# Loading q four tokens to a partition in a retention and MLP kernel

## The chip, the cores and the metric

The kernel runs on one core of a Trainium2 chip. The metric is the device time of one execution in microseconds (us); the median of several executions is used. The core has a matrix engine (PE), a vector engine (DVE), an engine for activations (ACT), a general one (POOL) and a queue engine (SP) that computes nothing and issues transfers. Each works through its own instructions in order; semaphores tie them together. Transfers are issued by SP, ACT or POOL and carried out by 16 DMA engines which all queues share.

## The reference: what is computed

```python
scores = scale * np.matmul(q, k.transpose(0, 1, 3, 2))        # scale = 1/8; q, k, v: [8, 8, 576, 64]
gamma = 1.0 - 2.0 ** (-5.0 - np.arange(H, dtype=np.float32))
rel = pos[:, None] - pos[None, :]
Dmat = np.where(rel >= 0, gamma[:, None, None] ** rel[None, :, :], 0.0)
attn = np.matmul(scores * Dmat[None, :, :, :], v)             # retention: causal, with a decay for each head
x = attn.transpose(0, 2, 1, 3).reshape(4608, 512)
h = x @ w_in                                                  # 512 -> 2048
out = (h * np.cos(h)) @ w_out                                 # 2048 -> 512
```

Inputs and output are float32; the kernel multiplies in bf16.

## The kernel before

**The retention part.** Each of 8 batches is cut into five pieces of 128 tokens (r = 0 to 3) and 64 (r = 4); here a pair (b, r) names one. Since the decay between two tokens is a product of a factor of the one and a factor of the other, q is multiplied by the table UQ, v by the table WV (`decay`, L311), and k is only cast to bf16 (`kcast`, L304). `load` (L273) brings k, q or v of a piece from memory into the float32 tiles kn, qn, vn: heads 0 to 3 lie in partitions 0 to 63, heads 4 to 7 in 64 to 127, and each partition holds ns consecutive tokens of a head (2, or 1 for r = 4). So a half of the load, one DMA, moves 64 partitions x 4 heads in runs of 512 bytes, and each load is two DMAs on SP (L281).

k and q of a piece must also stand with the 64 head elements in the partitions. In batches 0 and 1 PE transposes them (`turn`, L338; ACT copies them out, L348); from batch 2 on one DMA transpose issued by SP does it (`prep_dma`, L326, issue at L332). `scores` (L372) multiplies k and q, 16 small matmuls to a piece, into two PSUM banks sc, and DVE multiplies them by a causal mask MK (L389). `rest` (L394) multiplies these by v and, for r > 0, adds q times the state of the pieces before (ps<-kqt,sb); then it adds the piece's own k times v for the state. ACT copies the result out of PSUM into XT (L439), where it stands with d_model in the partitions and the tokens side by side: here the order of the tokens is put right. `state` (L444) adds to the float32 state on DVE (L453) and makes its bf16 copy on ACT (L456).

**The MLP part.** The 4608 tokens are nine blocks of 512. `mlp1` (L466) makes a block's 16 tiles of hidden values on PE, their cosine on ACT (L482) and the product on DVE (L485). `layer2` (L584) multiplies by w_out in seven products of 2 x 2 sub-blocks (fewer products, more sums on DVE), and stores.

**What sets the order.** The order is written out by hand in `emit` (L678). The start (L680 to L792) treats batches 0 and 1 and the first blocks. It issues all loads of batch 0, builds constants (`consts`, L227), and fills PE with matmuls on zeros (`idle`, L366) where it would wait, 12 of them first. The four loads of w_in and four of w_out are on POOL's queue; the first waits for v of (0, 0), the second for q of (0, 2), the third for q of (0, 3). From then on block j's `mlp1` tiles alternate with `layer2`. The retention of batch j+1 is put into the products of `layer2(j)` at the steps VISITS = 0, 3, 6, 9, 12: at each, `rest` of the piece before and `scores` of the next. The preparation is earlier: `prep_dma` of batch j+1, r = 2, 3, 4, in the `mlp1` tiles of block j and of batch j+2, r = 0, 1, in `layer2(j)`. In each, POOL casts k and multiplies q and v (L308, L317), SP issues the transpose, and then `loads_to` (L671) puts behind it on SP the next loads in order, so that before the transpose of (b, r) the loads of pieces 0 to 5b + r + 2, that is 5b + r + 3 pieces, have been issued, at least the 15 issued before the first transpose.

**Constants.** POOL's iotas write the token numbers IP and the differences MI for the mask (L239), DVE corrects the upper half (L243) and compares for the mask (L251); DVE zeroes the identity matrix and POOL puts in the ones (L246); ACT's exponentials make UQ and WV, one for each table and head, 16 in all (L260). PE's first transposes need the identity matrix, the first q decay (on DVE) needs UQ.

Of the kernel before, what the change touches and what calls it, by code (L numbers as in the profile page):

```python
# [6 lines left out]
ALU = mybir.AluOpType  # L7
# [7 lines left out]
NP = H_ // 2  # L15
# [28 lines left out]
def ns_of(r):  # L44

    return ck_of(r) // 64


# [92 lines left out]
class _Kernel:  # L141
    def __init__(self, nc, es, q, k, v, w_in, w_out, out):
# [52 lines left out]
        self.bOSB = [Buf() for _ in range(4)]  # L195
        self.IP = sb("ip", [128, NIP], F32)
        self.WV = sb("wv", [128, NIP * 4], F32)
        self.UQ = sb("uq", [128, NIP * 4], F32)
# [6 lines left out]
        self.C_PIH = sb("c_pih", [128, 1], F32)  # L205
        self.bIP, self.bWV, self.bUQ, self.bMK, self.bC, self.bID, self.bIDLE = (Buf() for _ in range(7))

# [19 lines left out]
    def consts(self):  # L227
        s = self.s
        s.op("dve", lambda e: e.memset(self.C_LN8.ap(), float(math.log(1.0 / 8.0))), writes=[Buf()])
        s.op("dve", lambda e: e.memset(self.C_PIH.ap(), float(math.pi / 2.0)), writes=[self.bC])  # L230
        s.op("dve", lambda e: e.memset(self.IDLE.ap(), 0.0), writes=[self.bIDLE])
        self.touch(AF.Exp)

        for t, b, o, n, pat, base, mul in (
                (self.IP, self.bIP, 0, NIP, [[CH, NCH - 1], [1, 2]], 0, 2),
                (self.IP, self.bIP, NIP - 1, NIP, [[0, 1]], CH * (NCH - 1), 1),
                (self.MI, self.bMK, 0, 2 * CH, [[-1, 2], [1, 2], [2, 64]], 0, -2)):
            shape = [[n, 128]] + [[1, 1]] if o else [[n, 128], [1, n - 1]] if n == NIP else [[n, 128], [128, 2], [64, 2], [1, 64]]
            s.op("pool", lambda e: e.iota(bass.AP(t, o, shape), pat, base=base, channel_multiplier=mul,  # L239
                                          allow_small_or_imprecise_dtypes=True), writes=[b])  # L240
        for o, n in ((0, NIP - 1), (NIP - 1, 1)):
            up = bass.AP(self.IP, 64 * NIP + o, [[NIP, 64], [1, n]])
            s.op("dve", lambda e: e.tensor_scalar(up, up, -128.0 if n > 1 else -64.0, None, ALU.add),  # L243
                 reads=[self.bIP], writes=[self.bIP])
# [12 lines left out]
        for t, b, sign in ((self.UQ, self.bUQ, 1.0), (self.WV, self.bWV, -1.0)):  # L257
            for h in range(H_):
                hs, hh = divmod(h, 4)
                s.op("act", lambda e: e.activation(  # L260
                    bass.AP(t, 64 * hs * 4 * NIP + hh, [[4 * NIP, 64], [4, NIP]]),
                    bass.AP(self.IP, 64 * hs * NIP, [[NIP, 64], [1, NIP]]), AF.Exp, scale=sign * self.lng[h],
                    **(dict(bias=bass.AP(self.C_LN8, 64 * hs, [[1, 64], [1, 1]])) if sign > 0 else {})),
                    reads=[self.bIP, self.bC], writes=[Buf()])
            b.w = [Tok("act", "act", s.count["act"], {})]

# [6 lines left out]
    def load(self, x, b, r, after=()):  # L273
        ns = ns_of(r)
        t, bt = self.ST32[x][r], self.bST32[x][r]

        def half(hs):
            dst = bass.AP(t, 64 * hs * 256 * ns, [[256 * ns, 64], [D_ * ns, 4], [1, D_ * ns]])
# [3 lines left out]

        return self.s.dma("sp", f"{x}n{r}", [half(0), half(1)], writes=[bt], after=after)

# [26 lines left out]
    def decay(self, eng, x, b, r):  # L311
        ns, i = ns_of(r), b % 2
        if x == "q":
            o, bt, w, bw = self.by_head(self.KQ[i][r], 256 * ns, 512 * ns, ns, D_, 256), self.bQB[i][r], self.UQ, self.bUQ
        else:
            o, bt, w, bw = self.by_head(self.VB[i][r], 0, 256 * ns, ns, D_ * ns, D_), self.bVB[i][r], self.WV, self.bWV
        self.s.op(eng, lambda e: e.tensor_tensor(  # L317
            o, self.by_head(self.ST32[x][r], 0, 256 * ns, ns, D_ * ns, D_),
            bass.AP(w, r * 8, [[4 * NIP, 128], [1, 4], [4, ns], [0, D_]]), ALU.mult),
            reads=[self.bST32[x][r], bw], writes=[bt])  # L320

# [50 lines left out]
    def scores(self, b, r):  # L372
# [3 lines left out]
        for c in range(2):  # L376
            for sl in range(ns):
                for hs in range(2):
                    for hp in range(2):
# [3 lines left out]
                            bass.AP(self.KQT[i], k0 + sl * 256, [[W, 64], [1, 64]]),  # L383
                            bass.AP(self.KQT[i], k0 + 256 * ns, [[W, 64], [256, ns], [1, 64]]),
                            dict(start=c == 0 and sl == 0, stop=c == 1 and sl == ns - 1, skip_group_check=True)))
        self.group(mms, [self.bKT[i][r], self.bQT[i][r]], self.bSC)
        for hp in range(2):
            p3 = [[512, 128], [ns * nq, 2], [1, ns * nq]]
            s.op("dve", lambda e: e.tensor_tensor(  # L389
                bass.AP(self.RT[r % 2][hp], 0, p3), bass.AP(self.SC[hp], 0, p3),  # L390
                bass.AP(self.MK, 0, [[2 * CH, 128], [0, 2], [1, ns * nq]]), ALU.mult),
                reads=[self.bSC[hp], self.bMK], writes=[self.bRT[r % 2][hp]])

    def rest(self, b, r, state=True):  # L394
# [39 lines left out]
        n0 = min(ck, XR - t0)  # L434
        for x0, po0, n in ((t0, 0, n0), (0, n0 // ns, ck - n0)):
            if n:
                o = bass.AP(self.XT, x0, [[NP * XR, 128], [XR, NP], [1, ns], [ns, n // ns]])
                p = bass.AP(self.PS, po0, [[1024, 128], [256, NP], [64, ns], [1, n // ns]])
                s.op("act", lambda e: e.activation(o, p, AF.Copy),  # L439
# [408 lines left out]
```

## Time and profile before

| | us |
|---|---|
| median of 3 runs | 309.16 (308.28 to 310.27) |
| the profiled execution's own time | 309.18 |
| its span, first to last instruction | 307.1 |
| PE busy | 292.3 |
| DVE busy | 232.3 |
| ACT busy | 190.1 |
| POOL busy | 115.8 |
| q's load issues on SP: 80, median of one | 0.617 |
| DMA transposes on SP: 30, median of one | 1.282 |

Times in the trace count from the start of the span. A line of a timeline gives the start, the time taken, the engine, the line of the kernel, the operation with its tiles, how many instructions were merged into it, and in brackets the idle time before it and what ended that. `SPq` is SP's queue; its issues are not counted as busy. A line of a source (L281 and so on) gives the least, the median and the longest time of one instruction in ns, then the first and last start. In a line of groups, the numbers after the first bar are the busy time in us and the mean of one instruction in ns, after the second bar the idle time of the engine just before and what ended it. Matmuls are pipelined, so that the time shown for one is longer than what it adds.

### The profile page before, as it was taken

What the parts mean: (1) busy time and instruction counts of PE and PEld (TensorE: products, weight loads), DVE (VectorE), ACT (ScalarE), POOL (GpSimd) and SP (SyncE); (2) the same over time, 40 slices, a digit from 0 to 9 for tenths busy, and PEclk for the clock granted to TensorE, in tenths of its full rate; (3) what the DMA queues carried; (4) which work ended last, traced back from release to release, by engine and by line L of the source; (5) the groups of instructions that cost most, each with busy time, mean ns of one, the idle gap of its engine ahead of it and who ended that gap; (6) DMA issues with size and microseconds to landing.
All of it is one profiled execution on the core that took longest, in us unless ns stands there. A gap on an engine that the chain in (4) does not pass through costs nothing.

```text
span 307.1 us, 8716 instructions
## 1 busy us (share of the span) xinstructions
PE 292.3 (95%) x3520; PEld 190.6 (62%) x3520; DVE 232.3 (76%) x393; ACT 190.1 (62%) x336; POOL 115.8 (38%) x133
## 2 busy tenths in 40 slices
PE   8768997999899999999999999999999999999996
PEld 3347644553587458746874687457845874685485
DVE  3347654867986898789878986999689768937963
ACT  6647845587565766576657665865576657724730
POOL 2346271999835444533551445436341000000000
PEclk9969999999999999999999999999999999999999
DMA  4999999567986987697879799977795012003003
GB/s 137 204 203 218 215 235 235 156 162 198 235 177 184 280 129 189 169 269 161 164 180 260 160 174 170 290 168 173 191 254 97 2 50 89 2 0 130 10 0 140
DMA packets 103480, 49.60 MB, mean 162 GB/s; under 512 B 45456, under 2 KB 98960, under 8 KB 103440
## 3 DMA queue, kind: packets, MB, share of 16 engines
q1 hardware_dynamic: 94176, 35.80, 54.2%
q10 hardware_dynamic: 5040, 9.05, 8.8%
q0 software_dynamic: 4224, 4.19, 8.4%
q8 instruction: 28, 0.46, 0.6%
q14 instruction: 12, 0.10, 0.1%
HBM read 36.70 MB, written 9.44 MB: 150 GB/s over the span
## 4 chain that ended last, share of the span: by engine, by line
PE 82%; DVE 5%; ACT 4%; SPq 4%; DMA 2%; issue 1%; POOL 0%; DVEq 0%; ACTq 0%
PE mm L362 59%; PE mm L364 14%; PE ps L362 6%; SPq L281 4%; PE sc L362 3%; DMA kn<-in_k_dram 2%; ACT cb L482 2%; DVE gt L485 1%; DVE ss L542 1%; DVE rt L389 1%; ACT sb L456 1%; ACT xt L439 1%; ACT kqt L348 1%; DVE ss L485 1%; DVE s L453 0%
## 5 line engine op out<-in xcount | busy, mean ns | idle before, releaser
L362 PE MATMUL mm<-xt,win 128*128 128x512 bf16 (+5 forms) x517 | 119.0, 349 | 2.0 <-DVE gt L485 1.2
L482 ACT ACTIVATE cb<-mm,c_pih 128x512 bf16<-128x512 f32 (+3 forms) x147 | 98.7, 680 | 33.7 <-PE mm L364 30.0
L485 DVE TENSOR_TENSOR gt<-mm,cb 128x512 bf16<-128x512 f32 (+1 forms) x130 | 85.7, 678 | 11.8 <-ACT cb L482 8.2
L362 PEld LDWEIGHTS mm<-xt,win 128*128 128x128 bf16 x517 | 46.8, 99 | 49.5 <-ACT cb L482 4.0
L364 PE MATMUL mm<-xt,win 128*128 128x512 bf16 (+5 forms) x147 | 54.0, 368 | 0.0
L389 DVE TENSOR_TENSOR rt<-sc,mk 128x512 bf16<-128x512 f32 (+1 forms) x80 | 44.8, 601 | 11.4 <-PE sc L364 11.4
L308 POOL CAST kq<-kn 128x512 bf16<-128x512 f32 (+1 forms) x40 | 25.2, 629 | 66.3 <-DMA kn<-in_k_dram 66.3
L317 POOL TENSOR_TENSOR kq<-qn,uq 128x512 bf16<-128x512 f32 (+1 forms) x37 | 36.9, 997 | 20.8 <-DMA qn<-in_q_dram 19.1
L362 PE MATMUL mm<-tt,ss 128*128 128x256 bf16 x336 | 43.2, 273 | 0.0
L439 ACT ACTIVATE xt<-ps 128x512 bf16<-128x512 f32 (+1 forms) x41 | 27.0, 661 | 24.6 <-PE ps L364 18.6
L317 POOL TENSOR_TENSOR vb<-vn,wv 128x512 bf16<-128x512 f32 (+1 forms) x34 | 34.4, 1013 | 17.1 <-DMA vn<-in_v_dram 14.4
L456 ACT ACTIVATE sb<-s 64x256 bf16<-64x256 f32 x64 | 26.6, 416 | 13.3 <-DVE s L453 12.1
L362 PEld LDWEIGHTS mm<-tt,ss 128*128 128x128 bf16 x336 | 31.4, 98 | 4.8
L566 ACT ACTIVATE sn<-mm 128x512 f32<-128x512 f32 x31 | 18.5, 598 | 25.1 <-PE mm L364 24.8
L542 DVE TENSOR_TENSOR ss<-gt 128x512 bf16<-128x512 bf16 (+1 forms) x56 | 32.1, 573 | 0.9
L571 DVE TENSOR_TENSOR osb<-mm,sn 128x512 f32<-128x512 f32 x30 | 20.6, 687 | 11.6 <-PE mm L364 11.3
L362 PE MATMUL mm<-wout,gt 128*128 128x256 bf16 x217 | 28.0, 273 | 0.3 <-DVE gt L485 0.3
L362 PE MATMUL mm<-wout,ss 128*128 128x256 bf16 (+1 forms) x160 | 27.4, 305 | 0.0
L453 DVE TENSOR_TENSOR s<-ps,s 128x256 f32<-128x256 f32 x24 | 10.2, 424 | 21.3 <-ACT xt L439 19.7
L364 PEld LDWEIGHTS mm<-xt,win 128*128 128x128 bf16 x147 | 14.4, 98 | 15.9
L362 PEld LDWEIGHTS mm<-wout,gt 128*128 128x128 bf16 x217 | 20.1, 98 | 4.1 <-DVE gt L485 0.5
L362 PEld LDWEIGHTS mm<-wout,ss 128*128 128x128 bf16 x160 | 15.1, 98 | 5.2
(76 smaller groups left out, 324.6 us busy)
## 6 DMA issues: line engine op xcount, KB each, us to landing
out_dram<-osb ACTq DMA_DIRECT2D x34, 256.0 KB, 3.4
kn<-in_k_dram SPq DMA_DIRECT2D x64, 128.0 KB, 3.4
qn<-in_q_dram SPq DMA_DIRECT2D x64, 128.0 KB, 3.4
vn<-in_v_dram SPq DMA_DIRECT2D x64, 128.0 KB, 3.7
win<-in_moe_w_in_dram POOLq DMA_DIRECT2D x4, 512.0 KB, 7.4
wout<-in_moe_w_out_dram POOLq DMA_DIRECT2D x4, 512.0 KB, 11.6
kn<-in_k_dram SPq DMA_DIRECT2D x16, 64.0 KB, 3.7
qn<-in_q_dram SPq DMA_DIRECT2D x16, 64.0 KB, 3.0
```

The costliest lines, as they stand in the source:

```text
L308: fn = (lambda e: e.activation(o, x, AF.Copy)) if eng == "act" else (lambda e: e.tensor_copy(o, x))
L317: self.s.op(eng, lambda e: e.tensor_tensor(o, self.by_head(self.ST32[x][r], 0, 256 * ns, ns, D_ * ns, D_), bass.AP(w, r * 8, [[4 * NIP, 12 ...
L362: self.nc.tensor.matmul(o, a, b, **kw)
L364: return s.done("pe", self.nc.tensor.matmul(o, a, b, **kw), reads, writes)
L389: s.op("dve", lambda e: e.tensor_tensor(bass.AP(self.RT[r % 2][hp], 0, p3), bass.AP(self.SC[hp], 0, p3), bass.AP(self.MK, 0, [[2 * CH, 128 ...
L439: s.op("act", lambda e: e.activation(o, p, AF.Copy), reads=[self.bPS], writes=self.bXT[x0 // GR:(x0 + n) // GR])
L456: s.op("act", lambda e: e.activation(bass.AP(self.SB[r % 2], 64 * hp * 512 + 64 * hp, [[512, 64], [128, NP], [1, D_]]), bass.AP(self.S32, ...
L482: s.op("act", lambda e: e.activation(ci, mi, AF.Sin, bias=self.C_PIH.ap(), scale=1.0), reads=[bm, self.bC], writes=[bcb])
L485: s.op("dve", lambda e: e.tensor_tensor(bass.AP(gt, dt * TB + o0, [[16 * TB, 128], [TB * step, k], [1, n]]), bass.AP(m, 0, [[512, 128], [n ...
L542: self.s.op(eng, lambda e: e.tensor_tensor(oo, xx, yy, op), reads=xb + yb, writes=ob)
L566: self.s.op("act", lambda e: e.activation(self.SN[k].ap(), bank[0].ap(), AF.Copy), reads=[bank[1]], writes=[self.bSN[k]])
L571: self.s.op("dve", lambda e: e.tensor_tensor(bass.AP(self.OSB, 2 * t * DM + 256 * h, [[4 * DM, 128], [DM, 2], [1, 256]]), bass.AP(bank[0], ...
```

## The change

q alone is loaded in another form. A partition now holds nj = 4 consecutive tokens (2 for r = 4) of two heads: heads 0 and 1 lie in partitions 0 to 31, heads 2 and 3 in 32 to 63, and so on. A load of q becomes four DMAs of 32 partitions x 2 heads in runs of 1 KB (512 bytes for r = 4) instead of two of 64 x 4 in runs of 512 bytes. Loads of k and v stay.

What follows from that order: UQ is made from token numbers IQ of its own, with one exponential for each of the two heads in a partition and the logarithm taken from a column of LG (six exponentials in all instead of 16, 16 memsets of one element, eight corrections on DVE instead of two, five iotas instead of three). The q columns of scores and of the state's product are read in runs of 32 instead of 64. The mask and the copy into XT use the new order of the tokens; the copy writes every fourth element instead of every second (every second instead of each one for r = 4).

The core of the diff (line numbers of the kernel before stand in the section above):

```diff
+def nj_of(r):
+
+    return ck_of(r) // 32
...
-                (self.MI, self.bMK, 0, 2 * CH, [[-1, 2], [1, 2], [2, 64]], 0, -2)):
+                (self.IQ, self.bIQ, 0, [[2 * NIP, 128], [4, NCH - 1], [1, 4]], [[CH, NCH - 1], [1, 4]], 0, 4),
+                (self.IQ, self.bIQ, 2 * NIP - 2, [[2 * NIP, 128], [1, 2]], [[1, 2]], CH * (NCH - 1), 2),
...
+                (self.MI, self.bMK, 0, [[2 * CH, 128], [128, 2], [32, 4], [1, 32]], [[-1, 2], [1, 4], [4, 32]], 0, -2)):
...
+        for h in range(H_):
+            for o, n, hd in ((0, 32, 2), (2, 64, 4)):
+                p, i = h // hd, h % hd
+                s.op("dve", lambda e: e.memset(bass.AP(self.LG, n * p * 6 + o + i, [[6, n], [1, 1]]),
+                                               self.lng[h] if o == 0 else -self.lng[h]), writes=[Buf()])
+        self.bLG.w = [Tok("dve", "dve", s.count["dve"], {})]
+        for t, b, n, w, o, c in ((self.IQ, self.bIQ, 32, 2 * NIP, 0, 2 * NIP - 2), (self.IP, self.bIP, 64, NIP, 0, NIP - 1)):
+            for p in range(1, 128 // n):
+                for o, m, k in ((0, c, CH), (c, w - c, 64)):
+                    up = bass.AP(t, n * p * w + o, [[w, n], [1, m]])
+                    s.op("dve", lambda e: e.tensor_scalar(up, up, -float(k * p), None, ALU.add),
+                         reads=[b], writes=[Buf()])
+            b.w = [Tok("dve", "dve", s.count["dve"], {})]
...
+        for t, bt, ip, bi, o, n in ((self.UQ, self.bUQ, self.IQ, self.bIQ, 0, 2),
+                                    (self.WV, self.bWV, self.IP, self.bIP, 2, 4)):
+            for i in range(n):
                 s.op("act", lambda e: e.activation(
+                    bass.AP(t, i, [[4 * NIP, 128], [n, 4 * NIP // n]]), ip.ap(), AF.Exp,
+                    scale=bass.AP(self.LG, o + i, [[6, 128], [1, 1]]),
+                    **(dict(bias=self.C_LN8.ap()) if o == 0 else {})),
+                    reads=[bi, self.bLG, self.bC], writes=[Buf()])
...
+        def quarter(g):
+            n = D_ * nj_of(r)
+            dst = bass.AP(t, 32 * g * 2 * n, [[2 * n, 32], [n, 2], [1, n]])
+            src = bass.AP(self.src[x], ((b * H_ + 2 * g) * S_ + CH * r) * D_, [[n, 32], [S_ * D_, 2], [1, n]])
+            return lambda e: e.dma_start(dst, src)
...
-        return self.s.dma("sp", f"{x}n{r}", [half(0), half(1)], writes=[bt], after=after)
+        parts = [quarter(g) for g in range(4)] if x == "q" else [half(0), half(1)]
+        return self.s.dma("sp", f"{x}n{r}", parts, writes=[bt], after=after)
...
         if x == "q":
+            o = bass.AP(self.KQ[i][r], 256 * ns, [[512 * ns, 128], [D_, 2], [128, nj], [1, D_]])
+            x = bass.AP(t, 0, [[256 * ns, 128], [D_ * nj, 2], [D_, nj], [1, D_]])
+            w, bw, bo = bass.AP(self.UQ, 8 * r, [[4 * NIP, 128], [1, 2], [2, nj], [0, D_]]), self.bUQ, self.bQB[i][r]
...
-                            bass.AP(self.KQT[i], k0 + 256 * ns, [[W, 64], [256, ns], [1, 64]]),
+                            bass.AP(self.KQT[i], 64 * hp * W + 1024 * r + 256 * ns + 32 * (2 * hs + c),
+                                    [[W, 64], [128, 2 * ns], [1, 32]]),
...
+            p3 = [[512, 128], [256, 2], [1, 256]] if ns == 2 else [[512, 128], [64, 2], [32, 2], [1, 32]]
+            mk = [[2 * CH, 128], [0, 2], [1, 256]] if ns == 2 else [[2 * CH, 128], [0, 2], [64, 2], [1, 32]]
...
-                     bass.AP(self.KQT[i], 1024 * r + 256 * ns + c * 128 + 64 * hs, [[W, 128], [256, ns], [1, 64]]),
+                     bass.AP(self.KQT[i], 1024 * r + 256 * ns + 32 * (2 * hs + c), [[W, 128], [128, 2 * ns], [1, 32]]),
...
-                o = bass.AP(self.XT, x0, [[NP * XR, 128], [XR, NP], [1, ns], [ns, n // ns]])
-                p = bass.AP(self.PS, po0, [[1024, 128], [256, NP], [64, ns], [1, n // ns]])
+                o = bass.AP(self.XT, x0, [[NP * XR, 128], [XR, NP], [1, nj], [nj, n // nj]])
+                p = bass.AP(self.PS, po0, [[1024, 128], [256, NP], [32, nj], [1, n // nj]])
```

More of the change, by code (lines that the diff above doesn't have):

```diff
@@ L205, in __init__ @@
         self.C_PIH = sb("c_pih", [128, 1], F32)
-        self.bIP, self.bWV, self.bUQ, self.bMK, self.bC, self.bID, self.bIDLE = (Buf() for _ in range(7))
+        self.bIP, self.bIQ, self.bLG, self.bWV, self.bUQ = (Buf() for _ in range(5))
+        self.bMK, self.bC, self.bID, self.bIDLE = (Buf() for _ in range(4))
         def ps(name):
@@ L256, in consts @@
             s.op("dve", lambda e: e.memset(self.SB[i].ap(), 0.0), writes=[self.bSB[i]])
-        for t, b, sign in ((self.UQ, self.bUQ, 1.0), (self.WV, self.bWV, -1.0)):
-            for h in range(H_):
-                hs, hh = divmod(h, 4)
+        for t, bt, ip, bi, o, n in ((self.UQ, self.bUQ, self.IQ, self.bIQ, 0, 2),
+                                    (self.WV, self.bWV, self.IP, self.bIP, 2, 4)):
+            for i in range(n):
                 s.op("act", lambda e: e.activation(
[L261 to L265, printed above, removed]
+                    bass.AP(t, i, [[4 * NIP, 128], [n, 4 * NIP // n]]), ip.ap(), AF.Exp,
+                    scale=bass.AP(self.LG, o + i, [[6, 128], [1, 1]]),
+                    **(dict(bias=self.C_LN8.ap()) if o == 0 else {})),
+                    reads=[bi, self.bLG, self.bC], writes=[Buf()])
+            bt.w = [Tok("act", "act", s.count["act"], {})]
     def touch(self, f):
@@ L434, in rest @@
         n0 = min(ck, XR - t0)
[L435 removed]
+        nj = nj_of(r)
+        for x0, po0, n in ((t0, 0, n0), (0, n0 // nj, ck - n0)):
             if n:
[L437 to L438 removed]
+                o = bass.AP(self.XT, x0, [[NP * XR, 128], [XR, NP], [1, nj], [nj, n // nj]])
+                p = bass.AP(self.PS, po0, [[1024, 128], [256, NP], [32, nj], [1, n // nj]])
                 s.op("act", lambda e: e.activation(o, p, AF.Copy),
```

31 lines of the change are left out of this document (13 added, 18 removed).

## The prediction

> **What bounds the kernel now.** I read the page's busy shares first, then the chain that ended last, then the SP queue, which section 1 of the page does not count as busy.
>
> ```profile
> PE 292.3 (95%) x3520; PEld 190.6 (62%) x3520; DVE 232.3 (76%) x393; ACT 190.1 (62%) x336; POOL 115.8 (38%) x133
> PE 82%; DVE 5%; ACT 4%; SPq 4%; DMA 2%; issue 1%; POOL 0%; DVEq 0%; ACTq 0%
> ```
>
> PE carries the chain, except at the start: there it runs through SP's load issues to 13.74 us and then through one landing.
>
> ```profile
> 13.74 7.09 DMA kn<-in_k_dram
> ```
>
> From 80 us on PE waits for almost nothing. The question is what stands just behind it. A piece is the load index r of a batch b: 128 tokens, or 64 for r=4. The timeline of SP alone shows one piece's turn, and the timelines of POOL and PE show the neighbours of the last transpose in it, which is that of batch 3, r=4.
>
> ```profile
> 116.81 1.27 SPq L332 DMA_TRANSPOSE kqt<-kq  x1
> 118.13 1.26 SPq L281 DMA_DIRECT2D kn<-in_k_dram  x2
> 119.43 1.71 SPq L281 DMA_DIRECT2D qn<-in_q_dram  x2
> 121.19 1.28 SPq L281 DMA_DIRECT2D vn<-in_v_dram  x2
> 122.56 1.38 SPq L332 DMA_TRANSPOSE kqt<-kq  x1
> ...
> 112.17 0.61 POOL L317 TENSOR_TENSOR vb<-vn,wv 128x256 bf16<-128x256 f32 x1 [0.77 <-DMA vn<-in_v_dram]
> ...
> 127.29 0.23 PE L362 MATMUL sc<-kqt 64*64 64x64 bf16 x7
> ```
>
> SP leaves gaps of 0.04 to 0.4 us and issues without other rest from 0.74 to 233.75 us. POOL was done with that piece at 112.78; its transpose was issued at 122.56, only because SP first had other issues in its queue. PE used the result 4.73 us after the issue, and a transpose lands 4.3 us (median) after it. So SP's issue time is the second bound, a microsecond or two behind PE, and it is exactly what the change touches. What one issue costs, by line (min/median/max ns):
>
> ```profile
> L281 SPq DMA_DIRECT2D qn<-in_q_dram x80: 595/617/2167, 2.2 to 227.7; - x80
> L492 ACTq DMA_DIRECT2D out_dram<-osb x34: 338/378/1083, 72.6 to 302.9; - x34
> L332 SPq DMA_TRANSPOSE kqt<-kq x30: 1227/1282/2208, 76.9 to 232.5; - x30
> ```
>
> **The change, part by part.**
>
> *q's issues.* Two per piece become four. Now: 2 x (0.617 + 0.04 gap) = 1.31 us of SP. No issue of 32 partitions x 2 runs of 1 KB is in the trace. Nearest rows: a load's half, 64 partitions x 4 runs (256 runs, least 595 ns; r=4's runs are half as long and cost the same), and a store, 128 partitions x 1 run (338 ns, the same at 1 KB and 2 KB). Three readings:
> - by all runs: 257 ns more for 128 more runs is 2.0 ns a run, so 64 runs cost 209 ns and a piece 4 x 0.249 = 1.00, or -0.32 us;
> - by runs to a partition (1 in the store, 4 in the load, 2 here): 338 + 257/3 = 424 ns, a piece 4 x 0.464 = 1.86, or +0.54 us;
> - by form alone (three dimensions, as the load): a piece 4 x 0.657 = 2.63, or +1.31 us.
>
> I take the middle one. The transpose speaks against the first: r=4's moves half the data and its issues still take 1.23 us against 1.28. The ends stay for the range.
>
> [...]
>
> *What +0.54 does.* From 81.70 to 229.78 SP handles 25 pieces, 5.92 us each; six loads and a transpose at their medians make 5.28, so 0.64 is issues that ran long. Two of six loads are q's, about 0.2 of that, and half may go with a quarter of the runs in each issue: net +0.45. SP's lateness at a transpose is 0.45 for each piece loaded before it. Of the first 15 I count only the four from 59.19 to 76.86, 1.8 us: from 26 to 56 SP's pairs took up to 3.9 us and the 16 DMA engines were at 1.0 to 1.2 of their time, so SP was waiting for them anyway. (If nothing is absorbed there, 15 x 0.45 = 6.8; if all is, 0.) Against it stands the slack between issue and use. (2,4), issued at 92.92, was used at 96.17 with no wait, so a half transpose lands within 3.25 us. The r=4 transposes have the least slack: issue 92.92, 122.56, 153.06, 182.64, 211.76 against use at 96.17, 127.29, 157.68, 188.08, 219.57, less 3.25: 0, 1.5, 1.4, 2.2, 4.6 us for batches 2 to 6. The load-ahead rule puts 2, 7, 12, 17, 22 pieces between batch 2's first transpose and these. PE's lateness: 2.7, 3.4, 5.8, 7.2, 7.1; batch 7 has 14 us of slack. These are not added: a PE held once uses the next one later too. The largest counts, +7.2 us. Who waits in that queue: the transposes behind the loads, for them PE's scores, and behind these the whole in-order PE. POOL gets its data later too, but has 10 us in hand.
>
> *Start.* The third k load is issued 3 x 0.54 = 1.6 later; it then lies 7.09 us behind busy engines, so it lands 0 to 1.6 late. POOL's first two weight loads wait in POOL's order for v's first and q's third landing (L289, 5.1 us in all) and go 0.5 and up to 1.6 later, with the k casts behind them. All this lies inside the +7.2 (PE late once is not late twice).
>
> *Packets.* q moves in 256 packets of 1 KB instead of 512 of 512 B. The queue of loads pays 29.9 ns a packet in the first 26 us (58.6% of 16 engines, 8160 packets), the stores' 2 KB packets 92 ns. By a straight line 1 KB costs about 51: 13.1 against 15.3 us of one engine, 0.14 us a piece over 16. Only the start can use it: -0.4 at most for three pieces.
>
> *Constants.* DVE gets 16 more memsets of one element (59 ns each, at most 90 apart: 0.9 to 1.4 us) and 6 more small adds (152 to 324 ns: 0.9 to 1.9) ahead of ident's memset at 1.84. POOL, with two more iotas (132 to 183 ns), then has ident 0.5 us later, at 4.2 to 5.6, and the k cast (now 4.65) at up to 5.6, 0.61 long. PE's idle matmuls cover to 5.92: 0 to 0.3 late. ACT has 6 exponentials instead of 16, from about 3.5; q's decay, now at 5.83, has its data 0.5 later anyway. Nothing, for the cover named.
>
> *Matmuls and mask.* The moving operand comes in four runs of 32 instead of two of 64. ps<-kqt,sb in two runs takes 220 ns, mm<-xt,win of 128 in one run 219: a run costs nothing. The mask's product (681 ns) keeps its elements; for r=4 (281 ns) its mask is read in runs of 32, at nothing by the same rows. q's decay (1101 ns on POOL) keeps 64-element runs.
>
> *The result's copy.* It writes every fourth bf16 element instead of every second. The rows by form:
>
> ```profile
> L439 ACT ACTIVATE xt<-ps 128x512 bf16<-128x512 f32 x31 | 23.2, 748 | 21.0 <-PE ps L364 15.1 <-PE sc L364 5.1
> L348 ACT ACTIVATE kqt<-mm 128x512 bf16<-128x512 f32 x8 | 4.8, 595 | 8.3 <-PE mm L364 8.3
> ```
>
> The step of two costs 153 ns over contiguous. A step of four: from 748 (no more) to 595 + 3 x 153 = 1054 (153 for each element stepped over); I take twice the excess, 900. What hides it: after the copy come DVE's sum and two ACT copies, ending 0.4 to 0.8 us before the next state product (122.54 against 122.96, 126.06 against 126.60). Cost 0; if that cover were gone, 24 x 0.15 = 3.6.
>
> [...]
>
> **Sum.** 309.18 (the profiled execution: span 307.1 and 2.1 around it; the median of the runs is 309.16) + 7.2 + 0.3 (constants, if not covered) = 316.7, about 317. Without absorption, 0.54 and 6.8 give +13; with 0.35 and 0 early, +3.8: its own range is 312 to 322.
>
> **Rivals.**
> - *Cheap issues, the other side.* Issue time goes with the runs: a piece is 0.32 us shorter, SP gains on PE, nothing of the steady part changes, since PE does not wait for it now. The third k load is up to 1 us earlier: 308.0 to 309.5, taken as 308.6. For it: 595 and 338 ns are nearly as 256 and 128 runs. Against it: the transpose. It decides from 0.29 us an issue downwards (4 x 0.33 = 1.31).
> - *Dear issues.* Form alone: +1.31 a piece, 1.1 net. A piece takes SP 7.0 us, a batch 35, over PE's 30.6 (113.0 to 143.7). At (6,4): 4 x 1.1 + 22 x 1.1 - 4.6 = +24: 333; unabsorbed to 340. For it: q keeps the loads' form and queue, and the transpose's cost hardly follows size.
> - *A shorter start.* Larger packets get through beside the weight loads, PE's wait of 13.75 to 16.70 shrinks and the half clock (0.50 at 18 to 24 us) does not come: up to 3 us of the 6 at half clock, 306. Against it: the loads in that wait are k and v.
> - *No change where it says.* The runs were 512 B before and nothing waits on q's transfer but POOL (19.1 us, hidden): this is the cheap case again.
>
> **How the numbers follow.** Forecast 0.36 (0.03 of it under 1%), dear 0.25, cheap 0.32 (0.03 of it slower by the copy), shorter start 0.07 (0.01 of it within 1%). One per cent, 3.1 us, is about what a measurement can tell here. Slower: 0.33 + 0.25 + 0.03 = 0.61; within: 0.03 + 0.29 + 0.01 = 0.33; faster 0.06. The time is the likeliest case's, 317; the range, 307.5 to 337, leaves out the short start and the top of the dear case.
>
> **What would show it.** Right: q's row at L281 x160 near 424 ns; SP pieces of 6.4 us; r=4's scores waiting for the transpose; the last load issued after 240 us. Wrong: q's issue at 0.29 us or less (then 309), or 0.6 (then 333). The copy's row at L439 shows its own price.

## The result, and the profile after

The changed kernel takes 329.25 us (median of 6 runs, 326.84 to 330.14), the kernel before 309.32 in the same six rounds (308.24 to 310.27): a ratio of 1.0639, 95% interval 1.0596 to 1.0681. That is 19.9 us more, where 7.8 were forecast. The profiled execution took 328.42 us, its span 326.6 (307.1 before, so +19.5), at the same mean granted clock, 0.989. Medians here and below are of all executions, while a ratio leaves out those that ran in a slower state of the chip, so that the two need not agree to the last digit.

In the changed kernel q's loads are issued at L301, those of k and v at L307, the transposes at L361; PE's matmuls stand at L391, the mask's product at L421, the result's copy at L472. First the page of the changed kernel, PE's line of section 1 and both lines of section 4 (shares of the span in the chain that ended last):

```profile
PE 294.0 (90%) x3496; PEld 189.6 (58%) x3520; DVE 231.0 (71%) x415; ACT 206.4 (63%) x326; POOL 114.1 (35%) x135
PE 65%; DVE 10%; ACT 9%; DMA 7%; SPq 5%; issue 3%; DVEq 0%
PE mm L391 45%; PE mm L393 11%; PE ps L391 6%; ACT xt L472 6%; DMA kqt<-kq 5%; DVE rt L421 5%; PE sc L391 3%; SPq L307 3%; DMA qn<-in_q_dram 2%; SPq L301 2%; ACT cb L515 2%; DVE gt L518 2%; DVE s L486 2%; ACT kqt L377 1%; DVE ss L575 1%
```

PE has as much to do as before (292.3 us), but no longer carries the chain alone: 82% has become 65%. The landing of transposes (kqt<-kq) is new in it, with 5%; the result's copy (xt) and the mask's product (rt) behind it have grown from 1% each to 6% and 5%. Next, what PE's matmuls and weight loads waited for (us in total, times, the longest):

```profile
PEld sc L391 <- DMA kqt<-kq: 12.7, 5, 4.7
PE sc L391 <- DMA kqt<-kq: 12.2, 5, 4.6
PEld ps L391 <- DVE rt L421: 6.0, 12, 0.5
```

PE now waits 12.7 us for transposes (the weight load and its matmul wait side by side, so these are not added), five times: 4.7 us at the scores of (2, 0), then 1.4, 2.6, 3.0 and 1.1 at those of r = 4 of batches 3 to 6. Before, it waited for none. It waits for the mask's product twelve times; before, once, 0.9 us. Why the transposes are late is seen on SP; here the turns that hold the last two transposes of batch 3, then the rows of the two lines (min/median/max in ns):

```profile
126.67 1.27 SPq L361 DMA_TRANSPOSE kqt<-kq  x1
127.98 1.88 SPq L307 DMA_DIRECT2D kn<-in_k_dram  x2
129.91 2.25 SPq L301 DMA_DIRECT2D qn<-in_q_dram  x4
132.21 1.32 SPq L307 DMA_DIRECT2D vn<-in_v_dram  x2
133.62 2.06 SPq L361 DMA_TRANSPOSE kqt<-kq  x1
```

```profile
L301 SPq DMA_DIRECT2D qn<-in_q_dram x160: 312/430/2010, 2.2 to 253.3; - x160
L361 SPq DMA_TRANSPOSE kqt<-kq x30: 1238/1285/2300, 83.4 to 257.9; - x30
```

The transpose of (3, 4) was issued at 133.62 instead of 122.56. From 87.56 to 255.13 SP handles 25 pieces: 6.70 us each, where it was 5.92. The whole of PE's path has taken that pace. The score groups that open batch 3 and batch 7, first in the kernel before, then in the changed one, from the timeline of PE:

```profile
112.35 0.39 PE L362 MATMUL sc<-kqt 64*64 64x128 bf16 x15
...
235.60 0.39 PE L362 MATMUL sc<-kqt 64*64 64x128 bf16 x15
```

```profile
120.32 0.39 PE L391 MATMUL sc<-kqt 64*64 64x128 bf16 x15
...
254.25 0.39 PE L391 MATMUL sc<-kqt 64*64 64x128 bf16 x15
```

Four batches took 123.25 us before, 30.8 each, and take 133.93 now, 33.5 each. Five pieces of SP are 29.6 before and 33.5 now. So before, SP was 1.2 us a batch faster than PE; now PE goes at SP's rate. Last, the row of the copy of 512 elements:

```profile
L472 ACT ACTIVATE xt<-ps 128x512 bf16<-128x512 f32 x31 | 40.8, 1316 | 18.1 <-PE ps L393 15.9 <-PE sc L393 1.4
```

1316 ns instead of 748. The prediction's highest value was 1054.

### The profile page after: what moved, and what is told of

Read it like the earlier page. It is cut to its first block, busy times and chain, and to the rows that moved or that the text cites. A ratio compares the mean times of both kernels' runs of the same rounds, so it can differ in the third digit from the quotient of the medians.

```text
span 326.6 us, 8743 instructions
## 1 busy us (share of the span) xinstructions
PE 294.0 (90%) x3496; PEld 189.6 (58%) x3520; DVE 231.0 (71%) x415; ACT 206.4 (63%) x326; POOL 114.1 (35%) x135
## 4 chain that ended last, share of the span: by engine, by line
PE 65%; DVE 10%; ACT 9%; DMA 7%; SPq 5%; issue 3%; DVEq 0%
PE mm L391 45%; PE mm L393 11%; PE ps L391 6%; ACT xt L472 6%; DMA kqt<-kq 5%; DVE rt L421 5%; PE sc L391 3%; SPq L307 3%; DMA qn<-in_q_dram 2%; SPq L301 2%; ACT cb L515 2%; DVE gt L518 2%; DVE s L486 2%; ACT kqt L377 1%; DVE ss L575 1%
## 5 line engine op out<-in xcount | busy, mean ns | idle before, releaser
L391 PE MATMUL mm<-xt,win 128*128 128x512 bf16 (+4 forms) x500 | 114.6, 345 | 3.1 <-DVE gt L518 1.4
L391 PEld LDWEIGHTS mm<-xt,win 128*128 128x128 bf16 x517 | 45.8, 98 | 50.6 <-DVE gt L518 5.1
L472 ACT ACTIVATE xt<-ps 128x512 bf16<-128x512 f32 (+1 forms) x41 | 45.7, 1121 | 21.8 <-PE ps L393 19.6
L421 DVE TENSOR_TENSOR rt<-sc,mk 128x512 bf16<-128x512 f32 (+1 forms) x80 | 44.8, 601 | 18.2 <-PE sc L393 18.2
L393 PE MATMUL mm<-xt,win 128*128 128x512 bf16 (+5 forms) x147 | 53.9, 367 | 0.4
L335 POOL CAST kq<-kn 128x512 bf16<-128x512 f32 (+1 forms) x40 | 24.5, 612 | 64.9 <-DMA kn<-in_k_dram 64.9
L349 POOL TENSOR_TENSOR vb<-vn,wv 128x512 bf16<-128x512 f32 (+1 forms) x34 | 33.6, 987 | 29.2 <-DMA vn<-in_v_dram 24.4
L391 PE MATMUL mm<-tt,ss 128*128 128x256 bf16 x336 | 43.2, 273 | 0.2 <-DVE ss L575 0.2
L599 ACT ACTIVATE sn<-mm 128x512 f32<-128x512 f32 x31 | 18.5, 597 | 26.9 <-PE mm L393 26.7
L391 PEld LDWEIGHTS mm<-tt,ss 128*128 128x128 bf16 x336 | 31.4, 98 | 5.0 <-DVE ss L575 0.3
L575 DVE TENSOR_TENSOR ss<-gt 128x512 bf16<-128x512 bf16 (+1 forms) x56 | 31.1, 555 | 0.9
L391 PE MATMUL mm<-wout,gt 128*128 128x256 bf16 x217 | 29.7, 283 | 0.0
L391 PE MATMUL sc<-kqt 64*64 64x128 bf16 (+1 forms) x536 | 15.0, 219 | 14.5 <-DMA kqt<-kq 12.2
L391 PE MATMUL mm<-wout,ss 128*128 128x256 bf16 (+1 forms) x156 | 26.5, 303 | 0.4 <-issue 0.3
L393 PEld LDWEIGHTS mm<-xt,win 128*128 128x128 bf16 x147 | 14.4, 98 | 15.9
L391 PEld LDWEIGHTS mm<-wout,gt 128*128 128x128 bf16 x217 | 20.8, 101 | 4.4 <-DVE gt L518 0.3
```

Source lines behind the costliest of these rows:

```text
L335: fn = (lambda e: e.activation(o, x, AF.Copy)) if eng == "act" else (lambda e: e.tensor_copy(o, x))
L349: self.s.op(eng, lambda e: e.tensor_tensor(o, x, w, ALU.mult), reads=[bt, bw], writes=[bo])
L391: self.nc.tensor.matmul(o, a, b, **kw)
L393: return s.done("pe", self.nc.tensor.matmul(o, a, b, **kw), reads, writes)
L421: s.op("dve", lambda e: e.tensor_tensor(bass.AP(self.RT[r % 2][hp], 0, p3), bass.AP(self.SC[hp], 0, p3), bass.AP(self.MK, 0, mk), ALU.mult ...
L472: s.op("act", lambda e: e.activation(o, p, AF.Copy), reads=[self.bPS], writes=self.bXT[x0 // GR:(x0 + n) // GR])
```

## The experiments

Two theories are told apart. Theory 1: the four issues of q make SP's queue slower than PE; the transposes behind them come later with every piece. Theory 2: the dear copy sets the time. All twelve kernels follow. The kernel before took 308.43 us (median of 7) beside the runs on issue times, copy alone, old copy and half of q; 309.21 (median of 13) beside q in four, transposes earlier, copies alone and q in one; 309.13 (median of 29) beside the other four.

### Issue times, shape by shape

The kernel holds nothing but DMAs of q's data on SP's queue, nine shapes (partitions x runs to a partition), eight in a row of each, then 64x4 and 32x2 by turns in pairs.

> Nothing of the reference is computed: SP issues eight loads of each of nine shapes from q, waits until they have landed, and goes on to the next shape; then two, two, two, two of 64 x 4 and 32 x 2 runs in turn; the output is filled with zeros. Time of one issue, by theory. All runs: 64 partitions x 4 runs 600 ns, 32 x 2 210, 32 x 4 340, 64 x 2 340, 128 x 4 1100, 128 x 1 340, 64 x 1 210, 32 x 1 145, 128 x 2 600. Runs to a partition: 64 x 4, 32 x 4 and 128 x 4 all 600; 64 x 2, 32 x 2 and 128 x 2 all 430; those with one run 340. Form alone: all with three dimensions 600, with two 340. In the changed kernel the first of q's four issues took 600 and the other three 430: if what was issued just before sets the first one's time, the turns of two show 600 at each first 32 x 2 after a 64 x 4 and 430 at the second.

Some rows (64x4, 32x2, 64x2, 128x4, 64x1, 32x1), min/median/max in ns. In the groups of 32x2, 64x2 and 128x4 the 16 DMA engines were near full (1.02, 1.01 and 0.90 of their time), and single issues ran long, most of all those of 32x2:

```profile
L690 SPq DMA_DIRECT2D dst<-in_q_dram x12: 601/624/1117, 0.7 to 83.6; - x12
L694 SPq DMA_DIRECT2D dst<-in_q_dram x12: 345/654/1084, 11.2 to 84.9; - x12
L702 SPq DMA_DIRECT2D dst<-in_q_dram x8: 602/619/848, 30.0 to 35.1; - x8
L706 SPq DMA_DIRECT2D dst<-in_q_dram x8: 403/507/1437, 39.0 to 43.7; - x8
L714 SPq DMA_DIRECT2D dst<-in_q_dram x8: 466/587/599, 59.1 to 63.8; - x8
L718 SPq DMA_DIRECT2D dst<-in_q_dram x8: 349/421/422, 66.5 to 69.7; - x8
```

And the turns at the end, from the timeline of SP:

```profile
80.51 1.32 SPq L690 DMA_DIRECT2D dst<-in_q_dram  x2
81.87 1.07 SPq L694 DMA_DIRECT2D dst<-in_q_dram  x2
82.99 1.26 SPq L690 DMA_DIRECT2D dst<-in_q_dram  x2
84.29 1.07 SPq L694 DMA_DIRECT2D dst<-in_q_dram  x2
```

None of the prediction's three readings holds. 512 runs on 128 partitions take 507 ns, 256 runs on 64 take 624: not the runs. One, two or four runs to a partition cost 0.59 to 0.62 on 64 partitions, and on 128 they go from 432 through 469 to 507 ns: the runs to a partition add little. Nor is it the form: 64x1 has two dimensions and takes 587, 128x4 has three and takes 507. What shows is 0.60 for an issue of 64 partitions, about 0.43 for one of 32 behind another of 32, and 0.60 for the first 32 behind a 64 (the pair's 1.07 us is 0.60 + 0.04 + 0.43). At the start of the changed kernel's trace the four issues of a q load indeed take 0.60, 0.42, 0.43 and 0.43.

### The copy alone

```diff
-        for x0, po0, n in ((t0, 0, n0), (0, n0 // ns, ck - n0)):
+        nj = 2 * ns
+        for x0, po0, n in ((t0, 0, n0), (0, n0 // nj, ck - n0)):
...
+                o = bass.AP(self.XT, x0, [[NP * XR, 128], [XR, NP], [1, nj], [nj, n // nj]])
+                p = bass.AP(self.PS, po0, [[1024, 128], [256, NP], [32, nj], [1, n // nj]])
```

> The kernel before, with the result's copy alone in the changed form (steps of four, read in runs of 32); the tokens within a piece come out in another order. Theory 1 (SP's issues hold PE through late transposes, the copy's cost is mostly covered): the copy takes 1.32 us as in the changed kernel, DVE's state sum and mask products come later, PE loses about 1 us a batch at the state's product: 312 to 316. Theory 2 (the copy is the main loss): 322 to 328.

316.73 us (median of 4), ratio 1.0271 [1.0222, 1.0320]: 8.3 us, by the copy and nothing else. The timeline shows how, from one copy to PE's next product; the wait's line closes it:

```profile
154.09 1.32 ACT L440 ACTIVATE xt<-ps 128x512 bf16<-128x512 f32 x1
...
155.51 0.42 DVE L454 TENSOR_TENSOR s<-ps,s 128x256 f32<-128x256 f32 x1 [1.59 <-ACT xt L440]
155.85 1.28 DVE L389 TENSOR_TENSOR rt<-sc,mk 128x512 bf16<-128x512 f32 x2
...
157.19 0.40 PE L362 MATMUL ps<-kqt,sb 128*128 128x128 bf16 x4 [0.23 <-DVE rt L389]
```

```profile
PEld ps L362 <- DVE rt L389: 5.0, 9, 0.9
```

The state's sum waits for the copy on DVE, and the two mask products stand behind it in DVE's order; PE then waits for them. The prediction followed the copy only to the state's own copies on ACT. PE's batch, measured as above, is 31.8 us instead of 30.8.

### The changed kernel with the old copy

The edit takes the copy's two access patterns back to those of the kernel before (`[1, ns], [ns, n // ns]` and `[64, ns]`), so that tokens stand in another order in the result.

> The changed kernel with the copy in the form of before (steps of two, runs of 64); the tokens within a piece come out in another order. Theory 1: transposes as late as in the changed kernel, 326 to 328; the copy's row back at 748 ns, waits of PE for the mask's product gone, waits for the transpose grown by as much. Theory 2: 311 to 314.

Ratio 1.0524 [1.0444, 1.0604], from two executions alone. With the copy at 746 ns most of the loss stays.

### The kernel before with q in four DMAs

```diff
+        def part(g):
+            dst = bass.AP(t, 32 * g * 256 * ns, [[256 * ns, 32], [D_ * ns, 4], [1, D_ * ns]])
+            src = bass.AP(self.src[x], ((b * H_ + 4 * (g // 2)) * S_ + CH * r + 32 * ns * (g % 2)) * D_,
+                          [[D_ * ns, 32], [S_ * D_, 4], [1, D_ * ns]])
...
+        parts = [part(g) for g in range(4)] if x == "q" else [half(0), half(1)]
```

> The kernel before with one edit: q's two DMAs of 64 partitions x 4 runs of 512 bytes become four of 32 partitions x 4 runs of 512 bytes. Runs, runs to a partition, the order of the tokens, the copy, the mask and every constant stay as before; only the number of issues and their 32 partitions change. Theory 1 in the form that the issue times by shape gave it (the first of four takes 0.60 us, the others 0.43): q's four take 1.9 to 2.0 us of SP instead of 1.31, as in the changed kernel, pieces come every 6.6 to 6.7 us, PE waits some 12 us for transposes, and the time is 323 to 328 us, as with the changed kernel with the old copy. Rival, the price goes by the runs to a partition (the reading that the prediction took, 617 ns each for four runs): 2.5 us a piece and over 333 us. Rival, theory 2 (the copy and the new order cost the time): about 308.5 us.

329.09 us (median of 4), ratio 1.0646 [1.0575, 1.0718]: as slow as the changed kernel, with nothing of it but q's four issues of 32 partitions. The row of q's issues, and PE's wait:

```profile
L287 SPq DMA_DIRECT2D qn<-in_q_dram x160: 311/432/1674, 2.2 to 255.3; - x160
```

```profile
PEld sc L369 <- DMA kqt<-kq: 15.2, 8, 4.1
```

Runs of 512 bytes, four to a partition, and still 432 ns, as with two of 1 KB (430).

### Transposes one piece earlier

```diff
-LEAD = 3
+LEAD = 2
...
-        self.loads_to(3 * NCH)
+        self.loads_to(2 * NCH + 3)
```

> The changed kernel with the loads one piece less ahead: LEAD is 2 instead of 3, and the batch of loads before the first transpose ends three pieces into batch 2 less two (2 x 5 + 3 pieces instead of 3 x 5). SP issues the same DMAs in the same number, but each transpose stands one or two pieces' loads (6 us each) earlier in its queue. Theory 1 (transposes come late because loads stand ahead of them on SP): the lines in which PE waits for the transposed q and k shrink from 12.8 us towards 0 to 4, and the time falls by 7 to 11 us to 318 to 322, about what the copy alone costs. What speaks against a full gain: the loads themselves come later, so that POOL may wait for them. Theory 2 (the slow copy makes the difference, and the waits for transposes only take the place of others): 327 to 330 us.

325.48 us (median of 4), ratio 1.0550 [1.0478, 1.0621]: 3.8 us less than the changed kernel, where I expected 7 to 11; the two intervals overlap, so that even this gain is not certain. SP's queue begins better and does not stay so:

```profile
72.18 4.01 SPq L361 DMA_TRANSPOSE kqt<-kq  x2
...
81.07 1.34 SPq L361 DMA_TRANSPOSE kqt<-kq  x1
...
129.19 1.24 SPq L361 DMA_TRANSPOSE kqt<-kq  x1
```

```profile
PEld sc L391 <- DMA kqt<-kq: 7.3, 5, 2.9
```

The first transpose is issued at 72.18 instead of 83.42, but that of (3, 4) at 129.19, only 4.4 us earlier, and PE waits for it again. The order of the queue shifts the transposes once; the rate at which SP works them off stays (34.0 us from one batch's last transpose to the next one's, 33.8 in the changed kernel). The miss sharpened theory 1 from "late" to "too slow".

### Half of q's issues taken away

```diff
-        parts = [quarter(g) for g in range(4)] if x == "q" else [half(0), half(1)]
+        parts = [quarter(g) for g in (range(4) if b == 0 else (0, 2))] if x == "q" else [half(0), half(1)]
```

> The changed kernel, in which from batch 1 on only two of q's four DMAs are issued (the first and the third); the other half of q is left out of the load and stays that of batch 0. Theory 1: a piece's q takes SP 0.60 + 0.43 + 0.08 = 1.1 us, less than the 1.31 before, so no transpose is late; what stays is the copy: 311 to 316, the same as the copy alone. Theory 2: 325 to 329.

314.48 us (median of 4), ratio 1.0171 [1.0103, 1.0240]. No wait of PE for a transpose is left. What remains is the copy's wait, and about the copy's price; the interval just meets that of the copy alone, [1.0222, 1.0320]:

```profile
PEld ps L391 <- DVE rt L421: 7.2, 15, 0.6
```

### Copies measured alone

A kernel with nothing but copies of one 128x512 block from PSUM to bf16, each form four times.

> No part of the reference's work: it leaves everything out but some copies of a 128x512 fp32 block of PSUM to bf16 in SBUF, each form four times in a row on one engine, by itself. On ACT: contiguous, written with a step of 2, of 4 and of 8 elements, written in runs of 32, and read with a step of 64 or 32 elements while the writes are contiguous in pairs or fours. On DVE: contiguous, step 2, step 4, and the read with a step of 32. Theory A (the step of the bf16 write sets the price, more with each doubling): contiguous 0.60 us, step 2 0.75, step 4 1.32, step 8 1.3 to 2.5; contiguous writes with a strided read stay near 0.60 to 0.75. Theory B (the price is of the access pattern's many short inner runs, wherever they lie): the strided reads cost as much as the strided writes. On DVE the block takes 0.6 to 1.4 us, and whether a step of 4 costs more there than a step of 2 says whether it is ACT's own.

On ACT written with a step of 1 (L703), 2 (L705), 4 (L707) and 8 elements (L709), and read with a step of 32 but written contiguously (L715); on DVE contiguous (L717), written with a step of 4 (L721), and read with a step (L723):

```profile
L709 ACT ACTIVATE xt<-ps 128x512 bf16<-128x512 f32 x4 | 9.7, 2432 | 0.1
L707 ACT ACTIVATE xt<-ps 128x512 bf16<-128x512 f32 x4 | 5.2, 1302 | 0.1
L721 DVE CAST xt<-ps 128x512 bf16<-128x512 f32 x4 | 5.2, 1290 | 0.1
L705 ACT ACTIVATE xt<-ps 128x512 bf16<-128x512 f32 x4 | 3.0, 738 | 0.1
...
L717 DVE CAST xt<-ps 128x512 bf16<-128x512 f32 x4 | 2.8, 691 | 27.4 <-ACT xt L715 27.3
L723 DVE CAST xt<-ps 128x512 bf16<-128x512 f32 x4 | 2.8, 691 | 0.1
...
L703 ACT ACTIVATE xt<-ps 128x512 bf16<-128x512 f32 x4 | 2.4, 597 | 0.4 <-PE ps L364 0.3
...
L715 ACT ACTIVATE xt<-ps 128x512 bf16<-128x512 f32 x4 | 2.4, 597 | 0.1
```

Theory A: the step of the write sets the price (597 to 2432 ns on ACT), and the step of the read from PSUM is free (597 ns, as contiguous). From two elements to four, and from four to eight, the time nearly doubles (738, 1302, 2432 ns). It is no straight line, as the prediction had drawn it. DVE pays about the same for a step of four (1290), so it is not ACT's own.

### The changed kernel with a copy that reads with the step

```diff
-                o = bass.AP(self.XT, x0, [[NP * XR, 128], [XR, NP], [1, nj], [nj, n // nj]])
-                p = bass.AP(self.PS, po0, [[1024, 128], [256, NP], [32, nj], [1, n // nj]])
+                o = bass.AP(self.XT, x0, [[NP * XR, 128], [XR, NP], [nj, n // nj], [1, nj]])
+                p = bass.AP(self.PS, po0, [[1024, 128], [256, NP], [1, n // nj], [32, nj]])
```

> The changed kernel with the result's copy walking PSUM with a step of 32 elements and writing bf16 contiguously, instead of reading contiguously and writing with a step of four elements. Expected copy: 597 ns by the copies measured alone, against 1316. The four issues of q stay. Theory 1, sharpened by the runs so far: from batch 3 on the kernel goes at SP's rate, 5 x 6.70 = 33.5 us a batch against PE's own 30.8 in the kernel before (score group (3, 0) to (7, 0), 123.3 us for four batches), and so a copy that is dear or cheap moves little: 325 to 328 us, PE's waits for transposes up to some 15 us. Theory 2 (the dear copy is the main cause): 309 to 315 us.

327.06 us (median of 4), ratio 1.0600 [1.0548, 1.0653]; the interval holds the changed kernel's 1.0639.

```profile
L472 ACT ACTIVATE xt<-ps 128x512 bf16<-128x512 f32 x31 | 18.5, 597 | 26.2 <-PE ps L393 24.4 <-PE sc L393 1.0
```

```profile
PEld sc L391 <- DMA kqt<-kq: 13.7, 7, 3.3
PEld ps L391 <- DVE rt L421: 1.6, 1, 1.6
```

The copy is 719 ns cheaper, the waits for the mask's product go from 6.0 to 1.6 us, and the median moves by 2.2 us, less than the intervals can tell: PE waits for the transposes instead. While SP sets the pace, the copy is covered.

### Both suspects taken away

The last edit, and half of q's issues left out from batch 1 on.

> The changed kernel with both suspects taken away: from batch 1 on two of q's four DMAs are left out (half of q is not loaded then, so the output is not the reference's), and the copy reads PSUM with a step and writes contiguously. Order of the tokens, mask, constants and matmuls are the changed kernel's. If the two suspects are all: the time of the kernel before, 307 to 310 us, or up to 2 us less since the copy is cheaper there than in the kernel before. Rival, something else in the change costs (stepped operands of the matmuls, the mask's form, the constants): 311 us or more.

308.39 us (median of 10), ratio 0.9994 [0.9965, 1.0022]. What PE waits for, of transposes or mask products, is this alone:

```profile
PEld ps L391 <- DVE rt L421: 1.7, 2, 1.6
...
PEld sc L391 <- DVE rt L421: 0.8, 2, 0.4
```

The stepped operands, the mask's new form and the constants cost nothing that can be measured. One limit: this kernel also saves a little against the kernel before, since it loads half of q (SP takes 28.9 us a batch against 29.7) and its copy takes 597 ns. The last kernel below is 0.5% faster by savings in these two places, so about as much could be hidden here. Beyond that the two suspects are all.

### The kernel before with savings in the same two places

Three kernels turn the findings round on the kernel before. The first has the copy of the last two, with `[64, ns]` read by step. The second loads q by one DMA of 128 partitions to a piece: the partition is twice the pair of tokens plus the half of the heads, and UQ's exponentials and the transposed q's columns follow that order. The third does both.

```diff
+        def whole():
+            dst = bass.AP(t, 0, [[256 * ns, 128], [D_ * ns, 4], [1, D_ * ns]])
+            src = bass.AP(self.src[x], (b * H_ * S_ + CH * r) * D_,
+                          [[D_ * ns, 64], [4 * S_ * D_, 2], [S_ * D_, 4], [1, D_ * ns]])
...
+        parts = [whole()] if x == "q" else [half(0), half(1)]
...
-                            bass.AP(self.KQT[i], k0 + 256 * ns, [[W, 64], [256, ns], [1, 64]]),
+                            bass.AP(self.KQT[i], k0 - 63 * hs + 256 * ns, [[W, 64], [256, ns], [2, 64]]),
```

> The kernel before with the copy alone turned round: PSUM read with a step of 64 elements, bf16 written contiguously, 597 ns expected against 748 in the kernel before. Theory 1 with its cover (the copy of the kernel before is covered by 0.4 to 0.8 us where a state sum follows): no difference that can be told, 308 to 310. Rival: each copy's 0.15 us is on the path as the dear copy's 0.57 was (8.4 us for 31 + 10 copies, about 0.4 of each copy's 0.57): up to 2.5 us less, 306.5 to 308.

> The kernel before with q loaded by one DMA of 128 partitions to a piece instead of two of 64: the partition is twice the pair of tokens plus the half of the heads, so that the transposed q's columns of one half of heads have a step of two. The copy and the mask are as before; q's decays come from four exponentials over 128 partitions. Theory 1: q's issue takes 0.5 instead of 1.31 us of SP, a piece 5.1 instead of 5.92, and the transposes come earlier; as PE does not wait for a transpose in the kernel before, that is worth nothing at the end: 307 to 310 us. Rival: the earlier loads help the start or POOL by 1 to 3 us, 305 to 307. Other way: the step of two in the moving q makes each score and state matmul dearer (222 ns now), or the one DMA lands later than two, 310 to 316.

> The kernel before with q in one DMA of 128 partitions and with the copy that reads with a step: a candidate against both kernels. SP's piece was 5.3 us with q in one, and the copy 597 ns. Theory 1: PE is the bound in the kernel before, so both savings lie beside it, 306 to 309 us. Rival: PE's own waits for sums and copies shrink by 2 us or more: 304 to 306.

The copy alone: 308.81 us (median of 12), ratio 0.9999 [0.9968, 1.0031]. q in one alone: 308.20 (median of 10), 0.9966 [0.9928, 1.0004]. Both: 307.21 (median of 12), 0.9952 [0.9927, 0.9977]. The row of q's issue in the second:

```profile
L313 SPq DMA_DIRECT2D qn<-in_q_dram x40: 615/617/1816, 2.2 to 213.2; - x40
```

One issue of 617 ns instead of two, not the 500 I expected from the shape in a row of its own kind; it stands behind k's 64 partitions, as the first 32 did. SP's batch falls to 27.7 us (5.5 a piece, not the 5.3 of the third kernel's expectation), and PE's stays at 30.8: the time that SP saves, which is not the bound here, gives nothing back that can be told. Both together are 0.5% faster than the kernel before, the only version here that beats both kernels, by about what can just be told.

## Why the prediction was wrong

The table puts the two rates beside each other: SP from the transpose of (2, 4) to that of (6, 4), PE from the scores of (3, 0) to those of (7, 0), each divided by four, in us for a batch.

| kernel | q's issues a piece | copy, ns | SP | PE |
|---|---|---|---|---|
| before | 2 | 748 | 29.7 | 30.8 |
| before, dear copy | 2 | 1320 | 29.9 | 31.8 |
| before, q in four | 4 | 745 | 34.0 | 33.8 |
| changed | 4 | 1316 | 33.8 | 33.5 |
| changed, copy reading by step | 4 | 597 | 33.5 | 33.9 |
| changed, transposes earlier | 4 | 1317 | 34.0 | 33.4 |
| changed, half of q | 2 | 1318 | 29.0 | 31.4 |
| changed, half of q, copy reading by step | 2 | 597 | 28.9 | 30.4 |
| before, q in one | 1 | 747 | 27.7 | 30.8 |

Within 0.6 us, PE's batch is the larger of its own 30.4 to 30.8 us (31.4 to 31.8 with the dear copy) and SP's. That carries 10.7 of the 18.7 us by which PE is late at the scores of (7, 0). The other 8.0 have come up by those of (3, 0), and only 5.0 of them at a wait for a transpose, that of the scores of (2, 0). Between the scores of (2, 0) and (2, 1) PE loses 1.7 more: right behind the long wait its products take nearly twice as long as in the kernel before, and the granted clock was 0.50 from 88 to 90 us (1.00 from 82 to 86 in the kernel before). The products of PE behind the scores of (2, 0), before and then changed:

```profile
82.15 0.93 PE L362 MATMUL mm<-wout,gt 128*128 128x256 bf16 x7
```

```profile
86.81 0.41 PE L391 MATMUL sc<-kqt 64*64 64x128 bf16 x15 [4.58 <-DMA kqt<-kq]
...
87.16 1.67 PE L391 MATMUL mm<-wout,gt 128*128 128x256 bf16 x7
```

The last 1.3 us come with waits for DVE; two of these, 0.5 us each, are for the mask's product behind the dear copy.

- **The mechanism was right.** SP's issue time was named as the second bound, the transposes behind the loads as what comes late, the r=4 transposes as the places, and PE as what waits. The row of q's issues came at 430 ns against 424 taken, the scores of r = 4 wait in batches 3 to 6, and the last load of q is issued at 253 us (after 240 forecast).
- **The step that failed: the size of SP's lateness.** Its first term, q's issue, was put at 424 ns for each of four, +0.54 a piece; the first of the four takes 0.60, and undisturbed the four took 1.96 to 2.06 us against 1.25 to 1.28 for two, +0.74. The next step took it down to +0.45, because smaller issues were to absorb part of the long ones. A piece went from 5.92 to 6.70: +0.78, and in sum nothing was absorbed. Three tenths of a us a piece are 7 us over 22 pieces. (By its own terms the upper end of its sum is 6.8 + 22 x 0.54 - 4.6 = +14, not +13.)
- **The early pieces.** Of the first 15 pieces the prediction counted four, 1.8 us, because, by its reading, SP waits for full DMA engines from 26 to 56 us (in that stretch they were at 1.17 of their time before, 1.18 in the changed kernel). The first transpose was 6.6 us late (83.42 against 76.86). The trace shows both halves: q's sixth load is issued 2.9 us late, the tenth, at 51.91, only 1.9 (absorbed in that stretch, as foreseen), and the fifteenth, at 80.03, 5.8: 3.9 us for five pieces, again near 0.8 each. What the first five pieces had built up was left out, and the later ones were priced at 0.45. So the longest wait, at (2, 0), was not in the prediction: the first transpose was issued at 76.86 and used at 81.80, it lands in 3.35 (83.42 to 86.76 in the changed kernel), and a slack of 1.6 covers nearly all of 1.8 but not 6.6.
- **The slack was right.** With the measured lateness of the r=4 transposes, 7.2, 11.1, 15.0, 19.6 and 23.7 us, less the prediction's slack of 0, 1.5, 1.4, 2.2 and 4.6, PE is late by 7.2, 9.6, 13.6, 17.4 and 19.1. It was late by 7.5, 9.7, 13.2, 17.0 and 18.5 at those scores. In batch 2 that is luck, since PE did not wait for this transpose: it was late from the wait at (2, 0), from the clock behind that, and from the copy. In the four others it did wait. There the form of the sum held; with +0.78 a piece and 6.6 at the start it gives the time. The rival of dear issues had this picture, a batch of SP over PE's 30.6, at a price too high (35 us a batch against 33.8).
- **The copy.** Taken at 900 ns, at most 1054; measured 1316, and its cover was not only the 0.4 to 0.8 us to the state's copies: the two mask products wait behind the state's sum on DVE. The cost "0, if the cover were gone 3.6" is 8.3 us in the kernel before. In the changed kernel little of it shows, because PE is held by SP there (1.0600 with the cheap copy, 1.0639 without); q in four alone gives as much as all of the change (1.0646 and 1.0639). So this step was wrong too, and the sum suffered little from it.
- **What was right beside it.** Matmuls (222 and 220 ns), the mask's product (681 and 281 ns) are as before; at the start the scores of (0, 1) come 1.8 us later (13.75 against 11.93), but by 30 us that is gone: a product of PE that began at 30.75 begins at 30.18. The 0.4 us by which PE is late at 35.5 stand behind a copy of 1.31 us in its chain, not behind constants or loads. The run with both suspects gone puts all these together at no more than some 0.5%.

## What to carry to other kernels

Compare rates before lateness: work out the queue's time for one round of the steady loop and the bound engine's time for the same round. Here a queue 4% faster than the engine it feeds (29.7 against 30.8 us a batch) was no cover for a change that added 13% to the queue (6.70 against 5.92 us a piece); every round then added its difference, and neither a head start (325.48 us against 329.25) nor a saving elsewhere (327.06) helped much. With the queue back at 28.9 us a batch and the cheap copy the loss was gone (308.39). And follow a slower instruction through everything behind it in the order of the next engine, not only through what uses its result.

## What the runs showed of the hardware

- The time of a load's issue on SP followed the partitions and the neighbour, and the runs only a little: 0.59 to 0.62 us for 64 partitions with one, two or four runs to a partition, 0.43 for 32 behind 32, 0.60 for 32 and 0.62 for 128 behind 64, and 0.43, 0.47 and 0.51 for 128 partitions with one, two and four runs behind their like. Why is open; no run here separates it further.
- Writing bf16 with a step: 597 ns contiguous, 738 at 4 bytes, 1302 at 8, 2432 at 16, for 512 elements in 128 partitions on ACT. Reading fp32 PSUM with a step of 32 or 64 elements cost nothing (597 and 598), so the same reordering is free on that side.
- Behind PE's wait of 4.7 us for the first transpose the granted clock was 0.50 (88 to 90 us in the changed kernel); behind its waits of 1.1 to 3.0 us in the same execution it stayed at 1.00. In the kernel with q in four, the mean granted clock was 0.96 from 80 to 120 us and from 120 to 160, where PE's scores waited for transposes three times up to 140 us, 7.2 us in sum, and 1.00 from 200 to 280 us, where they waited four times, 6.4 us in sum. What decides between these is open.
